# Attention and a bilinear feed-forward on one core: six passes instead of four transpose their exponentials on TensorE

## The chip, the core and the metric

One core of a Trainium2 chip runs the whole program. Its engines work side by side, each through its own queue in order: TensorE (PE; its weight loads are listed as PEld), VectorE (DVE), ScalarE (ACT), GpSimd (POOL), and SyncE (SP), which issues the transfers. The metric is the device time of one execution in microseconds. The kernel before takes 824.36 us (median of three runs, 823.71 to 825.22).

## The reference

```python
# q, k, v: (4, 8, 1152, 64) float32; two neighbouring query rows are averaged
q_pool = q.reshape(4, 8, 576, 2, 64).mean(axis=3)
scores = np.matmul(q_pool, k.transpose(0, 1, 3, 2)) / 8
attn = np.exp(scores - scores.max(-1, keepdims=True))
attn = attn / (attn.sum(-1, keepdims=True) + 1e-9)
x = np.matmul(attn, v)                      # (4, 8, 576, 64) -> 2304 tokens x 512
out = ((x @ w_a) * (x @ w_b)) @ w_out       # w_a, w_b: 512 x 1536, w_out: 1536 x 512
```

Everything is float32 at the interface. Inside, most factors of a product are split into a high and a low float16 part, and three of the four partial products are summed.

## The kernel before

**Passes.** Heads are handled in pairs, four pairs to a batch. A pass takes one pair through a set of query rows. In the first batch the rows are divided: passes 0 to 3 take pairs 0 to 3 through the 256 "even" tokens, passes 4 to 7 take pairs 3, 2, 1, 0 through the remaining 64 + 256 "rest" and "odd" tokens. In the other three batches a pass takes a pair through all 576 rows. A pass consists of units: two blocks of 128 query rows, one for each head, or a single narrow block in which 64 rows of either head share the 128 partitions. Passes 0 to 3 have two full units, passes 4 to 7 a narrow one and two full ones.

**A block.** `qk` forms 1152 scores a row on TensorE into the PSUM area `sps` (L699). `sm_max` on VectorE brings them to the tile `s` with the row maximum (L734), `sm_exp` on ScalarE takes the exponential and its sum (L741), `sm_sum` and `sm_rec` on VectorE give the reciprocal. There are two ways on from there.

**The float16 way** (passes 4 and later): `sm_hi` (ScalarE, L754) and `sm_lo` (VectorE, L758) write the normalised row as two float16 parts, a DMA transposes both (L763), and `pv` (L857) multiplies the 9 chunks of 128 keys with the split V, 54 matmuls for a full unit and 54 half as wide for a narrow one. V is split once a pass by `v_hi` (ScalarE, L541) and `v_lo` (VectorE, L544).

**The float32 way** (passes 0 to 3, `ps_.pe`, set by `n < N_PE`): `tr_pe` transposes the exponentials on TensorE, a chunk of 128 x 128 at a time, four chunks (or two, in the last part) to a part, into one of the two PSUM banks `ab0`, `ab1` (L776). `tr_out` brings each part back to SBUF, by turns on ScalarE (L787) and VectorE (L789). `pv_f` multiplies with the unsplit float32 V into the bank `xps` (L820); this shows as 36 matmuls for a full unit. `r_diag` (ScalarE, L792) puts the reciprocals on a diagonal, `r_wide` (TensorE, L796) spreads them over the partitions, also into `xps`, and `x_copy` (L870) and `r_mul` (L800) make the output of the unit. `xps` is one resource: a unit's products, the next unit's products and the sums of the weights' magnitudes go through it one after another.

**Weights.** `prep_w(f)` prepares one of 12 slices f of the three weight matrices: load, `w_abs` (L573) and `w_tail` (L592) on ScalarE, `w_sign` on GpSimd (L596), `w_join` on VectorE, a magnitude (`w_mag`, on ScalarE for odd f, L582), a sum over partitions on TensorE (`w_sum`, L615), and the high and low parts (`w_hi` L639, `w_lo` L643, L648, L652). The preparation is entered with the passes: three slices after each of passes 0 to 3 (`W_PASSES`).

**Expert tiles.** `moe_tile(t)` takes 256 tokens through the feed-forward: for each f two groups of 12 matmuls into `ab0` or `ab1` (`moe_mm`, L944), scaled and multiplied by `moe_a` (L951) and `moe_g` (L956), then a split by `moe_gh` (ScalarE, L961) and `moe_gl` (GpSimd, L964) and the output product (`moe_o`, L983). Tile 0 needs the even tokens of the first batch, whose last part comes from `x_hi` and `x_lo` of pass 3 (ScalarE L894, GpSimd L898). The banks `ab0` and `ab1` are also those of the transposes.

**What sets the order.** The body only enters tasks, by `add`, each with the tiles it reads and writes; a task is known by its number in the order of entry. `ORDERS` holds five lists, written out, that give each engine's sequence of task numbers, in the order TensorE, VectorE, ScalarE, GpSimd, SyncE; `Plan.order` merges them, and the instructions are issued in that sequence. An engine never passes over a task that waits. In the lists of before, task 491 is `x_hi` of pass 3 (172nd on ScalarE), tasks 579 and 575 are the first two products of expert tile 0 (103rd and 104th on TensorE), and task 24 is the first exponential.

## Time and profile before

| | |
|---|---|
| profiled execution | 824.24 us, span 822.5 us |
| TensorE busy | 781.4 us (95%), granted clock 0.980 on the mean |
| VectorE, ScalarE, GpSimd busy | 615.6, 581.6, 248.2 us |
| chain that ended last | TensorE 75%, ScalarE 9%, VectorE 9%, DMA 3% |

The 40 slices of the page, 20.6 us each, in tenths of a slice; PEclk is the clock that TensorE was granted, in tenths of 2.4 GHz:

```profile
PE   8887569999999999999999999999999999999997
DVE  5988999887799889999998999989887433022110
ACT  6999989877877878887987788788857442233212
PEclk9989789999999999999999999999999999999999
```

A row of the timeline gives the start in us, the time of the merged instructions, engine, line, operation, output <- inputs, the count, and in brackets the idle time before with what ended it. Matmul ends are modelled and successive instructions overlap a little, so the price of an operation is read from its start to the start of the next one. After the last matmul some 4 us are left for the last copy and store, and the profiled execution's time is 1.74 us above its span.

### The profile page before, as it was taken

What the parts mean: (1) busy time and instruction counts of PE and PEld (TensorE: products, weight loads), DVE (VectorE), ACT (ScalarE), POOL (GpSimd) and SP (SyncE); (2) the same over time, 40 slices, a digit from 0 to 9 for tenths busy, and PEclk for the clock granted to TensorE, in tenths of its full rate; (3) what the DMA queues carried; (4) which work ended last, traced back from release to release, by engine and by line L of the source; (5) the groups of instructions that cost most, each with busy time, mean ns of one, the idle gap of its engine ahead of it and who ended that gap; (6) DMA issues with size and microseconds to landing.
All of it is one profiled execution on the core that took longest, in us unless ns stands there. A gap on an engine that the chain in (4) does not pass through costs nothing.

```text
span 822.5 us, 21332 instructions
## 1 busy us (share of the span) xinstructions
PE 781.4 (95%) x8880; PEld 604.8 (74%) x8880; DVE 615.6 (75%) x1180; ACT 581.6 (71%) x986; POOL 248.2 (30%) x226
## 2 busy tenths in 40 slices
PE   8887569999999999999999999999999999999997
PEld 5664347776777767778778777887688788888886
DVE  5988999887799889999998999989887433022110
ACT  6999989877877878887987788788857442233212
POOL 5668866234201133211232023101310230311203
PEclk9989789999999999999999999999999999999999
DMA  8555698999999999999999989999968414000100
GB/s 300 209 198 174 198 212 245 190 214 218 203 202 220 208 190 190 204 212 192 190 215 203 174 177 168 209 162 213 161 117 154 88 43 100 2 27 1 27 2 26
DMA packets 316433, 132.32 MB, mean 161 GB/s; under 512 B 300848, under 2 KB 302896, under 8 KB 316336
## 3 DMA queue, kind: packets, MB, share of 16 engines
q1 hardware_dynamic: 316336, 130.96, 76.5%
q8 instruction: 69, 1.13, 0.5%
q14 instruction: 28, 0.23, 0.1%
HBM read 50.72 MB, written 4.72 MB: 67 GB/s over the span
## 4 chain that ended last, share of the span: by engine, by line
PE 75%; ACT 9%; DVE 9%; DMA 3%; issue 2%; POOL 0%; SPq 0%; ACTq 0%; DVEq 0%
PE ab L944 32%; PE ab L983 11%; PE xps L857 10%; PE sps L699 8%; PE sps L702 7%; PE sps L983 3%; DVE s L734 3%; DMA pt<-p 2%; ACT s L741 2%; DVE p L758 2%; ACT p L754 1%; PE xps L820 1%; PE xps L983 1%; ACT pt L787 1%; DMA xt<-in_w_ab_dram 1%
## 5 line engine op out<-in xcount | busy, mean ns | idle before, releaser
L944 PEld LDWEIGHTS <-wab 128*128 128x128 f16 x2592 | 251.4, 98 | 31.6 <-issue 0.9
L944 PE MATMUL ab<-xt,wab 128*128 128x256 f16 x2304 | 260.5, 273 | 0.6 <-DVE g L956 0.4
L741 ACT ACTIVATE s<-s,st 128x1152 f32<-128x1152 f32 x144 | 179.9, 1249 | 28.0 <-DVE s L734 27.2
L758 DVE SCALAR_TENSOR_TENSOR p<-s,st,p 128x1152 f16<-128x1152 f32 x128 | 183.6, 1438 | 15.3 <-ACT p L754 14.8
L754 ACT ACTIVATE p<-s,st 128x1152 f16<-128x1152 f32 x128 | 159.2, 1249 | 41.6 <-DMA pt<-p 14.4
L964 POOL TENSOR_TENSOR gl<-g,gh 128x256 fp32r<-128x256 f32 x108 | 90.0, 838 | 319.6 <-ACT gh L961 292.3
L699 PE MATMUL sps<-k,q 64*128 64x512 f32 (+3 forms) x448 | 101.5, 546 | 12.6 <-DVE s L734 6.5
L951 ACT ACTIVATE g<-ab,cc 128x256 f32<-128x256 f32 (+1 forms) x144 | 55.0, 415 | 82.6 <-PE ab L944 82.0
L734 DVE TENSOR_SCALAR_CACHE_REDUCE s<-sps,ksc 128x1152 f32<-128x1152 f32 x72 | 101.0, 1409 | 12.7 <-PE sps L702 12.2
L857 PEld LDWEIGHTS <-vs 128*64 128x64 f16 x3888 | 100.4, 110 | 13.6 <-issue 11.6
L956 DVE SCALAR_TENSOR_TENSOR g<-ab,cc,g 128x256 f32<-128x256 f32 (+1 forms) x144 | 55.3, 410 | 73.6 <-ACT g L951 73.3
L857 PE MATMUL xps<-pt,vs 128*64 128x128 f16 (+1 forms) x3888 | 109.1, 215 | 1.3 <-DMA pt<-p 1.0
L983 PE MATMUL ab<-wo,gh 128*128 128x512 f32 x336 | 108.9, 405 | 0.0
L734 DVE TENSOR_SCALAR_CACHE_REDUCE s<-sps 128x1152 f32<-128x1152 f32 x72 | 96.7, 1349 | 14.5 <-PE sps L699 13.8
L699 PEld LDWEIGHTS sps<-k,q 64*128 64x128 f32 (+1 forms) x448 | 47.1, 183 | 66.9 <-issue 50.9
L961 ACT ACTIVATE gh<-g 128x256 fp32r<-128x256 f32 x108 | 43.9, 411 | 52.8 <-PE ab L983 28.8
L983 PEld LDWEIGHTS ab<-wo,gh 128*128 128x128 f32 x336 | 60.4, 188 | 13.5 <-ACT gh L961 0.3
L983 PE MATMUL ab<-wo,gl 128*128 128x512 f32 x168 | 66.6, 396 | 1.0 <-POOL gl L964 1.0
L702 PE MATMUL sps<-k,q 64*128 64x512 f16 (+3 forms) x624 | 65.6, 341 | 1.9 <-DVE s L734 1.6
L702 PEld LDWEIGHTS <-q 64*128 64x128 f16 (+1 forms) x720 | 36.9, 97 | 41.0 <-issue 8.3
L596 POOL TENSOR_SCALAR xt<-xt 128x512 f16<-128x512 f32 x22 | 52.3, 2378 | 26.3 <-ACT xt L592 21.3
L424 POOL TENSOR_TENSOR q<-qraw 128x576 f32<-128x576 f32 (+2 forms) x20 | 28.0, 1402 | 61.0 <-DMA qraw<-in_q_dram 23.4
(135 smaller groups left out, 809.6 us busy)
## 6 DMA issues: line engine op xcount, KB each, us to landing
k<-in_k_dram SPq DMA_DIRECT2D x18, 576.0 KB, 4.4
vraw<-in_v_dram SPq DMA_DIRECT2D x17, 576.0 KB, 4.8
xt<-in_w_ab_dram SPq DMA_DIRECT2D x15, 512.0 KB, 3.9
qraw<-in_q_dram SPq DMA_DIRECT2D x12, 576.0 KB, 4.8
out_dram<-o SPq DMA_DIRECT2D x16, 256.0 KB, 2.9
xt<-in_w_out_dram SPq DMA_DIRECT2D x7, 512.0 KB, 3.9
g<-in_w_ab_dram SPq DMA_DIRECT2D x5, 512.0 KB, 3.2
wab<-in_w_ab_dram SPq DMA_DIRECT2D x4, 512.0 KB, 3.8
```

The costliest lines, as they stand in the source:

```text
L699: nc.tensor.matmul(out, q, k, start=True, stop=True)
L702: nc.tensor.matmul(out, q[:, hq], k[:, hk], start=(hq, hk) == (0, 0), stop=(hq, hk) == (1, 0))
L734: nc.vector.tensor_scalar(out=s_t[sbuf(i)], in0=sps[:, at:at + S], scalar1=-1.0 / 16.0 if u is None else ksc[:, u, 4:5], scalar2=None, op0 ...
L741: nc.scalar.activation(out=s, in_=s, func=AF.Exp, scale=-1.0, bias=t[:, 0:1], accum_out=t[:, 1:2])
L754: nc.scalar.activation(out=p_t[pbuf(i)][:, 0], in_=s_t[sbuf(i)], func=AF.Copy, scale=st_t[i % NST][:, 3:4])
L758: nc.vector.scalar_tensor_tensor(out=p[:, 1], in0=s, scalar=st_t[i % NST][:, 3:4], in1=p[:, 0], op0=ALU.mult, op1=ALU.subtract)
L857: nc.tensor.matmul(xps[half(e), at:at + w], vs[:, c, e, hv], pt[t][:, hp, c, c0:c0 + w], start=(c == 0 and n == 0), stop=(c == NCH - 1 and ...
L944: nc.tensor.matmul(dst if t < 8 else dst.rearrange("p (b n) -> p b n", b=B), wab[:, f, 1 - m, a, c], moe_x(t, b, c), start=(n == 0), stop= ...
L951: nc.scalar.activation(out=g_t[:, f, c], in_=ab[j][:, 1, c], func=AF.Copy, scale=cc[:, b, f, 0:1])
L956: nc.vector.scalar_tensor_tensor(out=g, in0=ab[j][:, 0, c], scalar=cc[:, b, f, 1:2], in1=g, op0=ALU.mult, op1=ALU.mult)
L964: nc.gpsimd.tensor_tensor(out=gl_t[j], in0=g_t[:, f], in1=gh_t[j].bitcast(F32), op=ALU.subtract)
L983: nc.tensor.matmul(out_bank(t, u), g[:, us], wo[:, f, a], start=(first and n == 0), stop=(last and n == 2))
```

## The change

`N_PE` goes from 4 to 6: passes 4 and 5 take the float32 way too. These have narrow units, so `r_wide`, `r_mul`, `moved` and `pv_f` get a width: a narrow unit has one block, nine chunks in three parts (ScalarE, VectorE, ScalarE bring them back), a product 64 columns wide, and a spread 64 wide. The spread reciprocals move from column 256 of `xps` to column 336 (`R_AT`). Pass 4 uses the float32 V of pair 3, which is still in `vraw`; pass 5 loads that of pair 2 into the place of the split V. The weights are entered over six passes, two slices with each. Tile 0 is entered after pass 5 (`m + 1 >= N_PE`), tile 1 after pass 7 as before. `moe_gl` of tiles 6, 7 and 8 is done on VectorE instead of GpSimd (`GL_DVE`). All five lists of `ORDERS` are new, and so are the numbers of the tasks: `x_hi` of pass 3 is now 413 (207th on ScalarE), the last eviction of pass 5 is 663, right behind it; the first products of tile 0 are 724 and 728 (145th and 146th on TensorE), and between them and the second halves stand 664 and 665, the last product and spread of pass 5. Of `ORDERS`, only lines with these numbers are shown.

```diff
@@ -25,12 +25,14 @@
 NF = DFF // 128
 NT = B * NQ
 P_SCALE = 2.0 ** 14
+R_AT = 336
 
 REMN = 64
 CC_F = 4
 IDLE = 8
 K_PART = 640
-N_PE, EVICT = 4, "ADADA"
+GL_DVE = (6, 7, 8)
+N_PE, EVICT = 6, "ADADA"
 N_WHOLE, TWO_ROUNDS = 2, (0,)
 
 XE, XR, XO = 0, 256, 320
@@ -52,164 +54,166 @@
 DMA_START, DMA_END, LOAD_LAG = 0.72, 0.63, 0.8
 Z_ALL, R_ALL = 30, 30
 W_KEY = (4, 1.3)
-W_PASSES = 4
+W_PASSES = 6
 PE_TICK, PE_WARM, PE_TURN, PE_STAY = 3.413, 1.275, 0.11, 0
 
 
 ORDERS = (
...
-        461, 462, 487, 488, 732, 508, 579, 575, 740, 580, 576, 750, 583, 584, 587, 534, 588, 758, 592, 593, 596, 597,
...
+        662, 638, 639, 836, 724, 728, 664, 665, 729, 725, 682, 846, 732, 736, 854, 733, 737, 871, 741, 742, 880, 745,
...
-        504, 702, 497, 433, 476, 463, 513, 725, 470, 431, 428, 489, 710, 491, 501, 507, 512, 524, 427, 728, 520, 734,
...
+        626, 620, 671, 594, 413, 663, 824, 590, 640, 647, 830, 678, 592, 653, 838, 677, 666, 833, 668, 687, 730, 726,
...
@@ -397,7 +401,7 @@
     vf = [vs.rearrange("p c e h d -> p (c e h d)").bitcast(F32).rearrange("p (c n) -> p c n", c=NCH), vraw]
 
     def vbuf(p):
-        return (["vsh", "vsl"], ["vraw"])[p % 2] if p < N_PE else ["vraw"]
+        return (["vsh", "vsl"], ["vraw"])[p % 2]
 
     pl = Plan()
     add = pl.add
@@ -528,7 +532,7 @@
         )
 
     def folds(ps_):
-        return ps_.p % NP == NP - 1 or ps_.p < NP and not ps_.pe
+        return ps_.p % NP == NP - 1 or ps_.p < NP and "odd" in ps_.parts
 
     def v_cc(b):
         nc.vector.tensor_scalar(
@@ -545,8 +549,9 @@
             out=vs[:, :, :, 1], in0=v_heads, scalar=vsc[:, p, 0:1], in1=vs[:, :, :, 0], op0=ALU.mult, op1=ALU.subtract
         )
 
-    def prep_vmax(p, new, key):
-        j = p % 2 if new and p < N_PE else 1
+    def prep_vmax(ps_, new, key):
+        p = ps_.p
+        j = p % 2 if ps_.pe else 1
         names = ["vraw"] if j else ["vsh", "vsl"]
         add("SP", 2.05, key - 3, load_v, (p, j), w=names, lag=LOAD_LAG)
         if new:
@@ -791,34 +796,39 @@
     def r_diag(i, e):
         nc.scalar.activation(out=diag[e], in_=ident, func=AF.Copy, scale=st_t[i % NST][:, 3:4])
 
-    def r_wide():
+    def r_wide(w):
         for e in range(2):
-            nc.tensor.matmul(xps[half(e), 256:384], one.broadcast_to([128, 64]), diag[e], start=True, stop=True)
-
-    def r_mul(j, x0):
-        x = x32[j][:, x0:x0 + 128]
+            d = diag[e] if w == 128 else diag[0][:, half(e)]
+            nc.tensor.matmul(xps[half(e), R_AT:R_AT + w], one.broadcast_to([128, 64]), d, start=True, stop=True)
+
+    def r_mul(j, x0, w):
+        x = x32[j][:, x0:x0 + w]
         nc.vector.scalar_tensor_tensor(
-            out=x, in0=x, scalar=1.0 / P_SCALE, in1=xps[:, 256:384], op0=ALU.mult, op1=ALU.mult
+            out=x, in0=x, scalar=1.0 / P_SCALE, in1=xps[:, R_AT:R_AT + w], op0=ALU.mult, op1=ALU.mult
         )
 
     def moved(ps_, i0, u):
-        parts = [[(i, c + d) for d in range(4)] for i in (i0, i0 + 1) for c in (0, 4)] + [[(i0, 8), (i0 + 1, 8)]]
+        both = (i0,) if u is None else (i0, i0 + 1)
+        parts = [[(i, c + d) for d in range(4)] for i in both for c in (0, 4)] + [[(i, 8) for i in both]]
+        u = u or 0
         out = []
         for n, chunks in enumerate(parts):
             j, w, on = (n + u) % 2, len(chunks), EVICT[n]
             of = sorted(set(i for i, _ in chunks))
-            name = f"pt{blocks[i0].slot}x{n}"
-            out.append(name)
+            names = [f"pt{blocks[i].slot}x{c // 4}" for i, c in chunks[::4 if w == 4 else 1]]
+            out += names
             add("PE", 0.04 + 0.11 * w, i0 - 6, tr_pe, (chunks, j), r=[f"s{sbuf(i)}" for i in of] + ["g0"], w=[f"acc{j}"])
-            add("ACT" if on == "A" else "DVE", (0.477 if w == 4 else 0.42) if on == "A" else (0.59 if w == 4 else 0.4), i0 - 3.5, tr_out, (chunks, j, on),
-                r=[f"acc{j}"], w=[name])
+            add("ACT" if on == "A" else "DVE", (0.477 if w == 4 else 0.42 if w == 2 else 0.25) if on == "A" else (0.59 if w == 4 else 0.4 if w == 2 else 0.2), i0 - 3.5, tr_out, (chunks, j, on),
+                r=[f"acc{j}"], w=names)
         return out
 
     def pv_f(p, at, slots):
+        w = 128 if len(slots) > 1 else REMN
         for c in range(NCH):
             for e in range(2):
+                c0 = 0 if len(slots) > 1 else REMN * e
                 nc.tensor.matmul(
-                    xps[half(e), at:at + 128], vf[p % 2][:, c, 64 * e:64 * e + 64], ptf[slots[e]][:, c],
+                    xps[half(e), at:at + w], vf[p % 2][:, c, 64 * e:64 * e + 64], ptf[slots[e % len(slots)]][:, c, c0:c0 + w],
                     start=(c == 0), stop=(c == NCH - 1),
                 )
 
@@ -880,7 +890,7 @@
         add("ACT", 0.072 + 0.192 * w / 256 + 0.08 * (ps_.pe or fold), key - 4, x_copy, (j, at, x0, w, ps_.p, ps_.pe, fold),
             r=["xps"] + [f"vb{ps_.p // NP}" if fold else f"vsc{ps_.p}"] * (ps_.pe or fold), w=[f"x32{j}{c}" for c in range(x0 // 64, (x0 + w) // 64)])
         if ps_.pe:
-            add("DVE", 0.2, key - 4, r_mul, (j, x0), r=["xps"], w=[f"x32{j}{c}" for c in range(x0 // 64, (x0 + w) // 64)])
+            add("DVE", 0.2, key - 4, r_mul, (j, x0, w), r=["xps"], w=[f"x32{j}{c}" for c in range(x0 // 64, (x0 + w) // 64)])
 
     def x_parts(p, j, which, hl):
 
@@ -960,8 +970,8 @@
     def moe_gh(f, j):
         nc.scalar.activation(out=gh_t[j], in_=g_t[:, f], func=AF.Copy)
 
-    def moe_gl(f, j):
-        nc.gpsimd.tensor_tensor(out=gl_t[j], in0=g_t[:, f], in1=gh_t[j].bitcast(F32), op=ALU.subtract)
+    def moe_gl(f, j, dve):
+        (nc.vector if dve else nc.gpsimd).tensor_tensor(out=gl_t[j], in0=g_t[:, f], in1=gh_t[j].bitcast(F32), op=ALU.subtract)
 
     sums_in = {}
 
@@ -1025,7 +1035,8 @@
             j = len(outs) % NG
             outs.append((t, f))
             add("ACT", 0.31, key - 20, moe_gh, (f, j), r=[f"g{f}"], w=[f"gh{j}"])
-            add("POOL", 0.7, key - 20, moe_gl, (f, j), r=[f"g{f}", f"gh{j}"], w=[f"gl{j}"])
+            dve = t in GL_DVE
+            add("DVE" if dve else "POOL", 0.36 if dve else 0.7, key - 20, moe_gl, (f, j, dve), port=True, r=[f"g{f}", f"gh{j}"], w=[f"gl{j}"])
             add("PE", 1.405, key - 1, moe_o, (t, f, j, f == 0, f == NF - 1),
                 r=[f"gh{j}", f"gl{j}", f"w{f}2h", f"w{f}2l"], w=sorted({out_name(t, u) for u in range(2)}), mode=3)
         for u in range(2):
@@ -1109,7 +1120,7 @@
     for n in range(IDLE):
         add("PE", 0.44, -40 if n < 8 else 2 * (n - 8), idle, (), r=["ones"], w=["xps"])
     prep_qk(passes[0], -20)
-    prep_vmax(0, True, -10)
+    prep_vmax(passes[0], True, -10)
 
     def attend(m):
         ps_ = passes[m]
@@ -1131,13 +1142,13 @@
                 block(ps_, i)
                 i += 1
             if r == 1 and nxt and not nxt.again:
-                prep_vmax(nxt.p, nxt.parts[0] == "even", ps_.end - 4)
+                prep_vmax(nxt, nxt.parts[0] == "even", ps_.end - 4)
             if ps_.pe:
-                parts = moved(ps_, i - 2, r)
-                add("PE", 2.02, i - 10, pv_f, (ps_.p, at, tuple(slots)), r=[f"pt{t}" for t in slots] + parts + vbuf(ps_.p),
+                parts = moved(ps_, i - 2, r) if w == 128 else moved(ps_, i - 1, None)
+                add("PE", 2.02 if w == 128 else 1.06, i - 10, pv_f, (ps_.p, at, tuple(slots)), r=[f"pt{t}" for t in slots] + parts + vbuf(ps_.p),
                     w=["xps"], mode=2)
-                add("PE", 0.3, i - 10, r_wide, (), r=["g1", "g2", "ones"], w=["xps"], mode=2)
-                leaving = [(at, XE + at, 128)]
+                add("PE", 0.3 if w == 128 else 0.17, i - 10, r_wide, (w,), r=["g1", "g2", "ones"] if w == 128 else ["g1", "ones"], w=["xps"], mode=2)
+                leaving = [(at, ps_.q0 + at, w)]
             else:
                 unit(slots, at, w, i - 1)
             for span in leaving:
@@ -1157,15 +1168,15 @@
             if ps_.p // NP == b:
                 attend(m)
                 if m < W_PASSES:
-                    weights(NF // W_PASSES * m, NF // W_PASSES * (m + 1))
-                if m == W_PASSES:
+                    weights(NF * m // W_PASSES, NF * (m + 1) // W_PASSES)
+                if m == W_PASSES - 1:
                     add("POOL", 0.4, ps_.base, kz_zero, (), w=["z2", "kz0", "kz1"], port=False)
                 if b and "even" in ps_.ends:
                     add("DVE", 0.1, NBLK * NP * b, v_cc, (b,), r=[f"wsc{f}" for f in range(NF)] + [f"vb{b}"],
                         w=[f"cc{b}{f}" for f in range(NF)])
                 for n in ps_.ends:
                     late.append(2 * b + (n == "odd"))
-                if b in TWO_ROUNDS:
+                if b in TWO_ROUNDS and m + 1 >= N_PE:
                     while late:
                         moe_tile(late.pop(0))
         while late and late[0] < 2 * b:
```

## Rows read from the trace of the kernel before

**Rows 1.** Busy time by stretch: length, PE, PEld, DVE, ACT, POOL, clock, DMA.

```profile
20.00:30.00 10.00, 9.60 (x88) 7.04 (x84) 9.61 (x25) 10.00 (x24) 3.48 (x3) 1.00 0.52 174
...
9.90:83.70 73.80, 62.19 (x465) 43.20 (x464) 66.20 (x145) 70.42 (x146) 54.64 (x29) 0.93 0.62 219
83.70:127.70 44.00, 28.12 (x224) 18.93 (x224) 42.28 (x87) 41.79 (x77) 34.90 (x18) 0.77 0.84 209
...
121.90:190.00 68.10, 66.81 (x886) 51.26 (x886) 61.22 (x109) 58.91 (x95) 25.90 (x19) 1.00 1.03 216
...
600.00:818.00 218.00, 218.00 (x2075) 184.53 (x2073) 71.97 (x168) 84.32 (x187) 42.39 (x56) 1.00 0.25 48
```

**Rows 2.** Timeline of PE: the first product of expert tile 0.

```profile
121.91 2.78 PE L944 MATMUL ab<-xt,wab 128*128 128x256 f16 x24
```

**Rows 3.** Timeline of ACT and POOL: first exponential, split of pass 3.

```profile
10.05 1.26 ACT L741 ACTIVATE s<-s,st 128x1152 f32<-128x1152 f32 x1 [0.28 <-DVE s L734]
...
119.98 0.41 ACT L894 ACTIVATE xt<-x 128x256 f16<-128x256 f32 x1
...
121.24 0.82 POOL L898 TENSOR_TENSOR xt<-x,xt 128x256 f16<-128x256 f32 x1
```

**Rows 4.** Timeline of PE in passes 0 and 1.

```profile
19.12 2.17 PE L699 MATMUL sps<-k,q 64*128 64x512 f32 x10 [0.16 <-issue]
21.23 1.09 PE L776 MATMUL ab<-g,s 128*128 128x128 f32 x8
22.25 2.19 PE L820 MATMUL xps<-pt,vs 128*64 128x128 f32 x36
24.27 0.39 PE L796 MATMUL xps<-g,one 128*64 128x128 f32 x4
24.59 0.44 PE L776 MATMUL ab<-g,s 128*128 128x128 f32 x2
24.96 0.48 PE L699 MATMUL sps<-k,q 64*128 64x128 f32 x2
25.37 0.66 PE L776 MATMUL ab<-g,s 128*128 128x128 f32 x4
```

**Rows 5.** Timeline of PE: a narrow and a full unit the float16 way.

```profile
155.65 1.04 PE L857 MATMUL xps<-pt,vs 128*64 128x64 f16 x54
156.62 1.48 PE L944 MATMUL ab<-xt,wab 128*128 128x256 f16 x12
...
164.62 1.70 PE L857 MATMUL xps<-pt,vs 128*64 128x128 f16 x54
166.25 2.15 PE L699 MATMUL sps<-k,q 64*64 64x512 f32 x12
```

**Rows 6.** Timeline of ACT in passes 3 and 4.

```profile
83.72 1.25 ACT L741 ACTIVATE s<-s,st 128x1152 f32<-128x1152 f32 x1
...
84.96 0.68 ACT L573 ACTIVATE wab<-wab 128x512 f32<-128x512 f32 x1
85.55 0.57 ACT L787 ACTIVATE pt<-ab 128x512 f32<-128x512 f32 x1
86.03 0.67 ACT L573 ACTIVATE o<-xt 128x512 f32<-128x512 f32 x1
86.60 0.39 ACT L792 ACTIVATE g<-g,st 128x128 f32<-128x128 f32 x1
86.89 0.66 ACT L592 ACTIVATE xt<-xt 128x512 int32<-128x512 uint32 x1
...
88.28 0.37 ACT L870 ACTIVATE x<-xps,vsc 128x128 f32<-128x128 f32 x1
88.53 0.67 ACT L573 ACTIVATE o<-xt 128x512 f32<-128x512 f32 x1
89.08 1.26 ACT L754 ACTIVATE p<-s,st 128x1152 f16<-128x1152 f32 x1
90.22 0.63 ACT L639 ACTIVATE wo<-o 128x512 fp32r<-128x512 f32 x1
```

286 rows, old and new, of the table ORDERS are left out of this document.

## The prediction

> **What bounds the kernel now.** I read the page's 40 slices first. From the seventh slice on TensorE stands at 9 and its clock at full speed; before that it stands at 5 to 8, while ScalarE and VectorE stand at 8 and 9. So there are two stages, and the table by stretch gives their limits. In the opening, from the first exponential to about 128 us, ScalarE is busy 70.42 + 41.79 = 112.2 of 117.8 us (95.3%), VectorE 66.20 + 42.28 = 108.5, TensorE 62.19 + 28.12 = 90.3, and part of that at 1.2 GHz: the granted clock is 0.93 and then 0.77 [rows 1]. From 121.9 to 190 us TensorE is busy 66.81 of 68.10 us at the full clock, at the end 218.0 of 218.0 [rows 1]. The border is the first product of expert tile 0, at 121.91 [rows 2]: behind it TensorE always has something to do.
>
> For this kernel that gives a simple account. Behind the first product of tile 0 the time is the sum of what then stands in TensorE's queue. In front of it the time is ScalarE's: that product needs the last part of x, which pass 3 splits on ScalarE at 119.98, and its low part on GpSimd, 0.82 from 121.24 [rows 3]. The change moves work from behind this border to in front of it, and it moves the border. The question is by how much each.
>
> **What leaves the queue behind the border.** TensorE's lists show it directly. Three scores, three remainders of scores and all six float16 units of passes 4 and 5 stood behind the first product and now stand in front of it (the units in their float32 form). Scores take 19.12 to 21.23 = 2.11 us, a remainder 24.96 to 25.37 = 0.41 [rows 4]; a full float16 unit 164.62 to 166.25 = 1.63, a narrow one 155.65 to 156.62 = 0.97 [rows 5]. That is 3 x 2.52 + 4 x 1.63 + 2 x 0.97 = 16.0. Only the last product of pass 5 and its spread stand behind the border anew: 22.25 to 24.27 = 2.02, and 24.27 to 24.59 = 0.32 [rows 4]. Net 16.0 - 2.3 = 13.7 us. So the change pays if the border moves by less than 13.7 us, to before 135.6.
>
> **What TensorE gets in all.** A full float32 unit costs four parts of four chunks at 0.51 (eight chunks take 21.23 to 22.25), one of two at 0.37, the product 2.02 and the spread 0.32: 4.75, against 1.63, so +3.12. The narrow unit is not in the trace. Its transposes are 2 x 0.51 and one chunk (0.13 to 0.37, I take 0.2); its product lies between half of the full one and all of it (1.01 to 2.02), and since the narrow float16 unit takes 0.97/1.63 of the full one I take 1.2; its spread lies between 0.16 and 0.32, I take 0.2: 2.6 in all, +1.65. Four and two of them make +15.8 (15.2 to 18.0) [rows 4, 5]. Nearly all of it stands in front of the border, where TensorE is not the limit. At full clock the work there was 62.19 x 0.93 + 28.12 x 0.77, less the 5.8 us behind the border: 73.7 [rows 1]. Now come 7.6 of scores, three full products with spreads (7.0), the transposes of four full units (9.6) and two narrow units (5.2): 103.1. If the border is near 136.7, that is 103 in 126.7 us: the cover holds if the mean granted clock of the opening is above 0.81.
>
> **What ScalarE gets in front of the border.** I counted its two lists from the first exponential to the split of pass 3. Prices are from start to start [rows 6]. Exponentials 22 to 27, 5 x 1.24 = 6.2. The float16 high parts, five of p and one of V, go: 6 x 1.14 = -6.8. Diagonals 16 to 24, 8 x 0.29 = 2.3. Four-chunk evictions 16 to 26, 10 x 0.48 = 4.8. Small evictions 8 to 13; I price them like the diagonal, 1.5 (0.25 to 0.48 each, 1.3 to 2.4). Copies of x 8 to 12, 4 x 0.25 = 1.0. One more split of x, of two parts, 0.6. Weights: 90 instructions to 99, 9 x 0.57 = 5.1. Sum +14.7. So although the passes themselves get cheaper for ScalarE, the border now waits for five more blocks and almost one more slice of weights. At the busy share of 95.3% [rows 1] this is 15.4 us: the split of pass 3 moves from 119.98 to 135.4. Its low part then starts about 0.4 later (before it stood behind another GpSimd instruction) and takes 0.82: the border comes at 136.6, which is 14.7 later than 121.91. The last eviction of pass 5, which frees the bank for the first product, stands right behind the split in the list and ends in the same half microsecond.
>
> **What I cost at nothing.** VectorE sheds ten low parts of p and two of V, and gains ten evictions and six products; it was less busy than ScalarE and stays so. Ten DMA transposes go; the DMA share was 0.62 to 0.84 there [rows 1], so no wait goes with them. The V of pass 5 goes to the other buffer, but is loaded as before. Each new product, spread, copy and multiplication goes through the one bank `xps`: behind a product that waits there stand, on TensorE, the scores of later blocks, and for these wait VectorE's maxima and ScalarE's exponentials. Passes 0 to 3 have the same chain, and its waits are inside the 4.7% that I keep; if it costs more, see the third rival. The subtractions of tiles 6 to 8 go to VectorE in a stretch where it is busy 72 of 218 us and TensorE never waits [rows 1]: no gain, no loss. Behind the border ScalarE still has weights to prepare: to the magnitude that the twelfth slice's sum needs are 5 exponentials, 6 high parts, 15 weight instructions and some 4 us of small ones, 25.6, at 95.3% 26.9: at 162.3. TensorE has 24.3 in front of that sum, and would be there at 160.9: a wait of some 1.4 us, against 1.29 us of idle that the stretch from 121.9 to 190 had [rows 1]. I count them as equal; the bounds are -2 and +4.
>
> **Sum.** The border +14.7, the queue behind it -13.7: +1.0. From the profiled execution's own 824.24 that gives 825.2 us; it was 0.12 below the median of the runs, 824.36.
>
> **The rivals.**
>
> First, ScalarE is held less, and the border comes early enough: faster. Of the way to the split of pass 3, some 5.2 us were idle. For it: VectorE was nearly as full, and it is what sheds work, so the waits on it could go; the new lists are another interleaving altogether. Against: TensorE, whose transposes ScalarE now waits for in six passes instead of four, gets fuller. If all the idle time goes, the border comes at 136.6 - 5.2 - 0.7 = 130.7, and the time is 819.3. It decides as soon as two thirds of it go: 136.6 - 4 is some 822.
>
> Second, the clock, which ends slower. Between 83.7 and 127.7 TensorE ran at a granted 0.77 [rows 1], that is nearly half the time at 1.2 GHz, after the idle stretches of a stage in which ScalarE set the pace. If the whole opening has that clock, 103.1 of work need 133.9 us, TensorE becomes the bound of its own border, which comes at 143.9, and the time is 832.5. It decides below 0.81, as worked out above. Against it: passes 0 to 3 did this kind of work at 0.93, and the stretch from 20 to 30 us, with transposes in it, at 1.00 [rows 1]; in the low stretch TensorE had little to do, and that is where the new work goes. The Trainium skill ("TensorE: Matmul & The Clock Gate", Part 4: PE-mode transpose) says that the full clock does not come on for transposes. By that rule the 90 new ones would run at 1.2 GHz and the clock would drop in passes 4 and 5; the trace of before does not agree, with its 1.00 between 20 and 30 us.
>
> Third, the chain through `xps` and the two banks holds ScalarE more than in passes 0 to 3, because six units instead of none now lie in the stretch behind 83.7. If its idle share doubles there, over some 53 us, the border comes 2.6 later: 827.8.
>
> **How the numbers follow.** A change of 0.2%, 1.65 us, is about what a measurement of this kernel can tell from none: below 822.7 is faster, above 826.0 slower. My forecast, ScalarE sets the border at its old busy share: 0.42, with a range of its own of 822.3 to 827.5 (its busy share two points either way; 0.03 of it faster, 0.25 the same, 0.14 slower). The first rival 0.34, all of it faster; the second 0.12 and the third 0.12, slower. Together: faster 0.37, same 0.25, slower 0.38. The range takes in the first rival with two microseconds less idle behind the border, and below the second's full price: 817.5 to 832.
>
> **What would show it.** In the profile after, the first L944 at 136 to 137, the pass 3 split (L894) 1.2 before it, ScalarE busy 95% up to there, and a granted clock above 0.86 in the opening show the steps right. L776 should have 234 matmuls instead of 144 and L754 118 instead of 128. The border before 133 with ScalarE busy 98% is the first rival; TensorE busy without a gap in the 50 us before its border, at a clock below 0.8, the second; ScalarE waiting for L796, L776 or L870's inputs the third. The account as a whole is wrong if the shift of the border less 13.7 is not the change in time: then the difference lies in waits behind the border, and the table by stretch will show where.

## The result: 0.8% slower, and the profile after

| | before | after |
|---|---|---|
| median of 5 runs | 824.36 us | 831.22 us |
| lowest to highest | 820.69 to 827.19 | 827.14 to 832.97 |
| ratio, 95% interval | | 1.0076, 1.0048 to 1.0103 |
| profiled execution, its span | 824.24, 822.5 | 832.97, 830.9 |

The time lies in the range (817.5 to 832), but the forecast of about the same time does not hold: the kernel got 6.9 us slower, the forecast was 0.8. The profiled execution of after is the longest of its five runs; the account below is of that execution (span +8.4). Two executions stand far out, 997.87 us of `tail_as_before` (an experiment below) and 1553.39 us of the kernel before in the second of the four sets there: the medians given hold them, the ratios do not.

The border first. The table of after by stretch (length, then PE, PEld, DVE, ACT, POOL, clock, DMA), with the opening, the 68.1 us behind the border, and the end, for [rows 1], and behind it the opening of before up to its own border:

```profile
10.17:138.10 127.93, 112.23 (x968) 76.75 (x968) 114.24 (x254) 121.16 (x259) 90.47 (x49) 0.93 0.55 192
138.10:206.20 68.10, 67.18 (x817) 50.88 (x817) 63.86 (x115) 59.40 (x98) 23.44 (x17) 1.00 1.00 212
...
600.00:818.00 218.00, 217.47 (x2226) 181.83 (x2224) 100.93 (x228) 94.11 (x198) 16.16 (x21) 1.00 0.34 62
```
```profile
10.00:121.91 111.91, 84.43 (x640) 57.33 (x640) 103.25 (x221) 106.82 (x213) 85.16 (x44) 0.86 0.69 212
```

Timelines of after: ScalarE's split of pass 3 and GpSimd's low part, for [rows 3]; TensorE's first product of tile 0 with what stands just ahead of it, for [rows 2]; and the new narrow float32 product, of which no row was to be had before:

```profile
135.97 0.41 ACT L904 ACTIVATE xt<-x 128x256 f16<-128x256 f32 x1
```
```profile
136.45 0.67 POOL L908 TENSOR_TENSOR xt<-x,xt 128x256 f16<-128x256 f32 x1 [1.82 <-ACT xt L904]
```
```profile
106.47 1.27 PE L830 MATMUL xps<-pt,vraw 128*64 128x64 f32 x36
107.57 0.29 PE L802 MATMUL xps<-g,one 128*64 128x64 f32 x4
...
124.98 4.10 PE L704 MATMUL sps<-k,q 64*64 64x512 f32 x12 [1.75 <-POOL q L428]
...
135.36 2.19 PE L830 MATMUL xps<-pt,vs 128*64 128x128 f32 x36 [0.35 <-DVE x L806]
...
138.11 2.79 PE L954 MATMUL ab<-xt,wab 128*128 128x256 f16 x24
```

The border moved by 16.2 us, from 121.91 to 138.11; 14.7 had been predicted. With the 13.7 us that left the queue behind it this makes +2.5, and a span of 825.0. The span is 830.9. The other 5.9 us came up behind the border. From here on I call that difference, span - (822.5 + shift of the border - 13.7), the **excess** of a run.

The table by stretch finds it. The next two fences have the same three stretches behind the border, of before and of after, and the third has the last of them for a kernel from the experiments (`after_to_p13`), with the same columns:

```profile
121.91:200.00 78.09, 75.81 (x972) 57.06 (x971) 67.89 (x119) 66.69 (x108) 32.67 (x25) 1.00 1.04 219
200.00:300.00 100.00, 98.51 (x1220) 73.75 (x1218) 84.91 (x152) 76.91 (x114) 19.17 (x21) 1.00 1.09 203
...
345.00:435.00 90.00, 88.73 (x1226) 68.74 (x1224) 86.54 (x153) 75.26 (x113) 18.37 (x19) 1.00 1.12 203
```
```profile
138.11:200.00 61.89, 61.55 (x747) 46.80 (x748) 58.24 (x106) 55.57 (x93) 23.43 (x17) 1.00 0.99 214
200.00:300.00 100.00, 99.42 (x1161) 73.61 (x1158) 86.24 (x157) 74.38 (x112) 20.44 (x23) 1.00 1.07 194
...
345.00:435.00 90.00, 84.61 (x1142) 64.96 (x1141) 81.34 (x148) 69.75 (x105) 21.20 (x20) 0.96 1.03 197
```
```profile
345.00:435.00 90.00, 88.27 (x1144) 69.30 (x1141) 77.11 (x137) 66.79 (x104) 16.60 (x19) 1.00 0.96 183
```

The idle time of TensorE is length less busy time. Up to 300 us before had 2.3 + 1.5 = 3.8 us of it, after has 0.3 + 0.6 = 0.9: the new lists are better there by 2.9. From 345 to 435 us before had 1.3, after has 5.4, and its clock is 0.96 instead of 1.00, worth an estimated 0.04 x 90 = 3.6 us. Nearly the whole loss lies in those 90 us: 4.1 + 3.6 - 2.9 makes 4.8 of the 5.9 us, and some 0.8 more are short waits behind 435 us. TensorE's timeline of after shows the place: two waits, 4.85 us in sum, and behind each of them work at a lower clock: 53 products of p and V take 2.95 us instead of 1.67, a score 2.81 instead of 1.62:

```profile
401.88 1.62 PE L707 MATMUL sps<-k,q 64*128 64x512 f16 x15
...
416.80 2.95 PE L867 MATMUL xps<-pt,vs 128*64 128x128 f16 x53 [2.58 <-DMA pt<-p]
...
430.31 2.81 PE L707 MATMUL sps<-k,q 64*128 64x512 f16 x15 [2.27 <-DVE s L739]
...
499.76 1.67 PE L867 MATMUL xps<-pt,vs 128*64 128x128 f16 x53 [1.74 <-DMA pt<-p]
```

VectorE in the same place (the timeline of after) is without a gap up to 417.8 and then stands still for 3.83 us, because the score that it needs next is queued on TensorE behind the product that waits for the transposes:

```profile
421.68 1.42 DVE L739 TENSOR_SCALAR_CACHE_REDUCE s<-sps,ksc 128x1152 f32<-128x1152 f32 x1 [3.83 <-PE sps L707]
```

### The profile page after: what moved, and what is told of

Same layout as the page of the kernel before. It is cut to its first block, busy times and chain, and to the rows that moved or that the text cites. A ratio compares the mean times of both kernels' runs of the same rounds, so it can differ in the third digit from the quotient of the medians.

```text
span 830.9 us, 21321 instructions
## 1 busy us (share of the span) xinstructions
PE 797.9 (96%) x8886; PEld 615.8 (74%) x8886; DVE 622.0 (75%) x1220; ACT 574.6 (69%) x1008; POOL 223.0 (27%) x190
## 5 line engine op out<-in xcount | busy, mean ns | idle before, releaser
L763 DVE SCALAR_TENSOR_TENSOR p<-s,st,p 128x1152 f16<-128x1152 f32 x118 | 167.6, 1429 | 22.5 <-ACT p L759 21.8
L759 ACT ACTIVATE p<-s,st 128x1152 f16<-128x1152 f32 x118 | 146.3, 1249 | 38.2 <-DVE st L756 18.8
L974 POOL TENSOR_TENSOR gl<-g,gh 128x256 fp32r<-128x256 f32 x72 | 68.3, 955 | 226.2 <-ACT gh L971 170.4
L867 PE MATMUL xps<-pt,vs 128*64 128x128 f16 (+1 forms) x3564 | 101.8, 216 | 5.5 <-DMA pt<-p 5.2
L867 PEld LDWEIGHTS <-vs 128*64 128x64 f16 x3564 | 93.8, 111 | 16.9 <-issue 15.6
L781 PE MATMUL ab<-g,s 128*128 128x128 f32 x234 | 38.0, 292 | 8.8 <-ACT pt L792 4.9
```

The lines of the kernel that those rows point to most:

```text
L759: nc.scalar.activation(out=p_t[pbuf(i)][:, 0], in_=s_t[sbuf(i)], func=AF.Copy, scale=st_t[i % NST][:, 3:4])
L763: nc.vector.scalar_tensor_tensor(out=p[:, 1], in0=s, scalar=st_t[i % NST][:, 3:4], in1=p[:, 0], op0=ALU.mult, op1=ALU.subtract)
L867: nc.tensor.matmul(xps[half(e), at:at + w], vs[:, c, e, hv], pt[t][:, hp, c, c0:c0 + w], start=(c == 0 and n == 0), stop=(c == NCH - 1 and ...
L974: (nc.vector if dve else nc.gpsimd).tensor_tensor(out=gl_t[j], in0=g_t[:, f], in1=gh_t[j].bitcast(F32), op=ALU.subtract)
```

## The experiments

Task names: P13u4pv is the product of p and V of unit 4 of pass 13, P14b94qk the score of block 94 in pass 14, P17ksum the broadcast of a maximum in pass 17, T2f5o the output piece of slice 5 of tile 2. Each engine has one written list of such tasks. A kernel that "changes over" at a task issues everything that after's order issues before that task in that order, and all the rest in the order of before. Ratios are to the kernel before, run on the same chip in the same set of runs; its medians were 823.68, 823.78, 823.97 and 824.14 in the four sets.

| kernel | median, us | ratio (95%) | border | excess |
|---|---|---|---|---|
| after_again | 830.85 | 1.0075 (1.0054 to 1.0096) | 137.5 | +4.9 |
| tail_as_before | 824.05 | 1.0000 (0.9985 to 1.0016) | 136.0 | -0.8 |
| gl_gpsimd | 829.54 | 1.0065 (1.0046 to 1.0085) | 133.5 | +6.2 |
| tr_twice | 828.76 | 1.0062 (1.0038 to 1.0086) | 136.1 | +7.9 |
| pv13_later | 829.83 | 1.0068 (1.0043 to 1.0092) | 136.9 | +4.5 |
| pv_both_later | 833.17 | 1.0098 (1.0073 to 1.0123) | 135.4 | +9.2 |
| qk26_later | 824.46 | 1.0006 (0.9992 to 1.0020) | 137.9 | -0.5 |
| abs_twice | 825.13 | 1.0018 (1.0005 to 1.0030) | 138.5 | -0.2 |
| after_to_p13 | 821.57 | 0.9967 (0.9952 to 0.9982) | 139.6 | -3.7 |
| after_to_p15 | 830.62 | 1.0064 (1.0042 to 1.0087) | 135.3 | +3.8 |
| lo_short | 827.99 | 1.0043 (1.0022 to 1.0063) | 133.5 | +4.4 |
| tr_half | 827.14 | 1.0042 (1.0022 to 1.0061) | 137.3 | +3.1 |

Border and excess are of the profiled execution, the median of all runs of the kernel. An excess is thus one sample: in the four kernels that leave after's order behind the border as it is up to 600 us (after, after_again, gl_gpsimd, tr_twice) it lies between 4.9 and 7.9.

**Where the loss is.** `after_again` is the kernel after the change, unchanged.

> The changed kernel unaltered, for a second profile. My theory: its time is the first product of expert tile 0 (138.1 us, 16.2 later than before, fixed by ScalarE's queue and the same from run to run within 0.5), plus a queue behind it that is 13.7 shorter, plus waits of TensorE behind it and the low clock after them, which vary: the profiled run had 8.9 us of waits and two stretches at half clock. So the border comes at 138 +- 0.5 again, and the time anywhere from 827 to 833, with the difference in waits and clock between 400 and 500 us. Rival: what is slower is fixed and sits in the opening; then the border itself moves with the time.

The ratio came again (1.0075), and so did the two waits: 2.61 us at 416.72 and 2.26 at 428.64. But behind the first of them the clock stayed up this time, 1.67 us in place of 2.95:

```profile
416.72 1.67 PE L867 MATMUL xps<-pt,vs 128*64 128x128 f16 x53 [2.61 <-DMA pt<-p]
```

`tail_as_before` keeps the six passes and the new opening, changes over at the first maximum of pass 10 (some 220 us) and leaves the low halves of the last tiles on GpSimd:

```diff
-lists of after
+lists of after up to P10b54max, then the order of before
-GL_DVE = (6, 7, 8)
+GL_DVE = ()
```

> The changed kernel up to the first maximum of pass 10 (some 220 us); from there on every engine works off what is left in the order of the kernel before, and the low parts of tiles 6 to 8 are on GpSimd again. Theory: the border stays at 138, the waits behind it fall to those of before (6.5 us, no low clock after 140 us), so the time is that of before plus 16.2 less 13.7, some 827, 4 us less than the changed kernel. Rival, the loss is the work that TensorE got in addition or the opening: 831, as the changed kernel. Rival, the order behind the border makes nothing but noise: 831 and as widely spread.

It takes as long as before, excess -0.8; that is 3 us less than the theory's 827, because the border came 2 us earlier than in after and TensorE idles 6.1 us behind it, against 7.1 before. So the six passes with their border cost what the account says, next to nothing, and the loss belongs to the order behind the border. `gl_gpsimd` has only the second half of that edit:

> The changed kernel with the low parts of tiles 6, 7 and 8 on GpSimd again, in the same place of the sequence. Theory: TensorE is full there, so only its end changes: within 1 us of the changed kernel, 830 to 831 for the median. Rival: VectorE, which gets 36 subtractions, holds the maxima of the last passes; then 3 us or more come back.

Excess 6.2, and a median 1.3 us below that of after_again: the subtractions on VectorE are not it.

**The opening.** `tr_twice` issues the transposes of passes 4 and 5 twice, into the same bank, so TensorE gets some 10 us more ahead of the border:

```diff
-        for n, (i, c) in enumerate(chunks):
-            nc.tensor.transpose(acc[j][:, 128 * n:128 * n + 128], ...
+        for again in range(2 if chunks[0][0] >= 16 and len(chunks) == 4 else 1):
+            for n, (i, c) in enumerate(chunks):
+                nc.tensor.transpose(acc[j][:, 128 * n:128 * n + 128], ...
```

> The changed kernel with every four-chunk part of passes 4 and 5 transposed twice: 20 parts of 0.51 us, 10.2 us more on TensorE in front of the border, same result. Theory, TensorE is covered there by ScalarE: the border comes at most 2 us later (each eviction waits half a microsecond longer, but ScalarE has other work in its queue), time +0 to +2. Rival, the added TensorE work is what the change pays for: the border comes 8 to 10 us later and the time is about 840.

The border stayed within what it varies by, far from the 8 to 10 us of the rival, so most of TensorE's share of the change is covered, as predicted. Not all of it: gl_gpsimd, with the same granted clock in the opening and without the added work, has its border at 133.5, 2.5 us earlier. The table by stretch of this kernel from 10 us to its border:

```profile
10.00:136.07 126.07, 114.61 (x1048) 83.31 (x1047) 111.60 (x254) 121.88 (x260) 87.52 (x49) 0.99 0.59 197
```

Eighty more float32 transposes, and the granted clock is 0.99. `abs_twice` adds to ScalarE instead, on the base of tail_as_before:

```diff
-        nc.scalar.activation(out=z_t[zi(n)], ..., func=AF.Abs, scale=2.0 ** -112)
+        for _ in range(2 if 18 <= n < 24 else 1):
+            nc.scalar.activation(out=z_t[zi(n)], ..., func=AF.Abs, scale=2.0 ** -112)
```

> The same kernel (824.05), in which six of the weights' magnitudes on ScalarE (experts 6 and 7) are computed twice, ahead of the border: 6 x 0.57 us = 3.4 us more on ScalarE, the output is unchanged. Theory (ScalarE sets the border at 95% busy, and what the border loses the end loses): border 135.96 + 2.5 to 3.4 = 138.5 to 139.4, time 826.5 to 827.5. Rival (ScalarE has slack where it waits 2.6 us for transposes just ahead of the border): border 136 to 137, time 824 to 825.

The border went to 138.5, 2.5 later, but the median only rose by 1.1 us: between the two expectations. The next kernel, without the added work, has its border at 137.9 at the same granted clock of the opening, 0.93. The kernel after (138.1) and tr_half (137.3), with the opening lists unaltered and at 0.93 too, have theirs in the same place. Only a small part of what ScalarE gets arrives at the border. `qk26_later`, on the same base, moves one score out of the way on TensorE (P5u0pvf is the float32 product of unit 0 of pass 5):

```diff
-... W9.1wsum P6b26qk P5u2tr0 P5u0pvf P5u0rwide P5u2tr2 ...
+... W9.1wsum P5u2tr0 P5u0pvf P6b26qk P5u0rwide P5u2tr2 ...
```

> The kernel with the six passes in the opening, the order of before behind it and the low halves of the last three tiles on GpSimd (824.05 in the earlier run), with one edit: in TensorE's list the first scores of the first float16 pass (P6b26qk) stand behind the last transposes of P5u2's first chunk and the narrow product P5u0pvf, no longer ahead of them. Theory (TensorE's 1.76 us wait for q on GpSimd at 122 to 124, half-clock scores of 3.6 us behind it and ScalarE's 2.6 us wait for the transposes behind those are a loss on the path to the border): ScalarE's wait at 125.4 falls below 1 us, the border comes 1.5 to 2.5 us earlier (133.5 to 134.5), time 822 to 822.8, below the kernel before. Rival (ScalarE's sum and the later products set the border anyway, the first maxima of pass 6 come later and hold it): border 135.5 to 136.5, time 824.

A miss, and the rival's account: ScalarE waits 4.3 us for a later maximum in place of 2.6 for the transposes, and the time is the same.

**Which wait it is.** My theory was one misplaced product, P13u4pv, too early in TensorE's list.

```diff
-... P13u2pv P13u3pv P13u4pv P14b94qk T2f5o P14b95qk ...
+... P13u2pv P13u3pv P14b94qk T2f5o P13u4pv P14b95qk ...
```

> The kernel after the change with one edit: in TensorE's written list the last attention product of pass 13 stands one score block and one output piece later (behind P14b94qk and T2f5o). Theory (the loss is two waits that the new order behind the border puts at 414 to 430 us, with the low clock that follows them): the 2.6 us wait of the attention product for the transposed p at 416.8 and the 2.3 us wait of the scores at 430.3 go, the clock in 400 to 440 is back near 1.00, the border stays at 136 to 138; the excess of the span over 822.5 + shift of the border - 13.7 falls from 5.9 to about 1 to 2, time 825 to 827. Rival (the moved border piece or VectorE's new load is what costs, and the waits only come up a few us later): waits behind the border stay at 8 to 9 us, excess 5 to 6, time 829 to 831.

The theory fell. In TensorE's timeline of pv13_later the wait for the transposes is gone and the clock is up, but three other waits of 5.0 us in sum stand in the same stretch:

```profile
416.06 1.65 PE L679 MATMUL sps<-k,q 64*64 64x512 f16 x18 [1.99 <-DVE s L711]
...
426.47 0.73 PE L965 MATMUL ab<-wo,gh 128*128 128x512 f32 x2 [2.23 <-ACT gh L943]
...
429.41 1.62 PE L679 MATMUL sps<-k,q 64*128 64x512 f16 x15 [0.77 <-DVE s L711]
```

The second edit of the kind, at 500 us, did not help:

```diff
-... P15u3pv P15u4pv P16b112qk P17ksum T3f0o P16b113qk ...
+... P15u3pv P16b112qk T3f0o P15u4pv P17ksum P16b113qk ...
```

> As the run before, and the last attention product of pass 15 also one score block and one output piece later (behind P16b112qk and T3f0o; the maximum's broadcast P17ksum goes behind it, since both write the same PSUM bank). Theory: the 1.7 us wait at 499.8 goes too; excess 0 to 1, time 823.5 to 826, 1 to 2 us below the run before. Rival: TensorE is not what sets the pace at 500 (VectorE waits 2 us for scores there anyway): no difference to the run before.

The wait at 499.8 goes and four of 0.7 to 0.8 us stand in its place. The median is 3.3 us above that of pv13_later, but the intervals of the two ratios overlap, and the excess of 9.2 is not the edit's alone: up to 435 us the two kernels have the same lists and the same three waits (here 2.07, 2.23 and 0.65), and behind the last of them the clock fell here and stayed up there:

```profile
427.61 3.04 PE L679 MATMUL sps<-k,q 64*128 64x512 f16 x15 [0.65 <-DVE s L711]
```

Then two changes of order as a whole. Both have GL_DVE = () and change over at another task: `after_to_p13` at P13b81max (some 345 us), `after_to_p15` at P15b99max (some 435 us).

> The written lists of the kernel after the change up to the first maximum of pass 13 (some 345 us), behind it the order of before, low halves of the last three tiles on GpSimd. Where the order changes over, the products of tile 2 that before's lists have had by then come in a bunch among the scores of pass 13. Theory (the loss is made at 400 to 500 us, where the lists of after give VectorE 97 to 98% of work and TensorE no expert product to do meanwhile; the order up to 345 us is as good as before's): border 133.5 to 138, TensorE waits at 400 to 500 us about 2 us as in the run with before's order from pass 10, excess of the span over 822.5 + shift of the border - 13.7 between -1 and +1, time 822 to 825. Rival (the loss is laid down earlier, by the expert products of tile 1 that stand later in after's lists than in before's at 220 to 345 us, and only shows at 400): excess 4 to 6, time 828 to 830.

> The same with the change-over at the first maximum of pass 15 (some 435 us): the stretch with the waits of 2.6 us at 416.8 and 2.3 us at 430 and the low clock between them is after's, that with the wait of 1.7 us at 499.8 is before's. Theory: the first two waits stand as in after and cost with the low clock 4 to 6 us, the third is gone: excess 3 to 5, time 826.5 to 829. Rival (the waits there are recovered later, the loss is made behind 435 us): excess 0 to 1, time 823 to 825.

With the stretch from 345 to 435 us in before's order the excess is -3.7; with the same stretch in after's it is +3.8, with both waits where they were:

```profile
414.69 1.67 PE L839 MATMUL xps<-pt,vs 128*64 128x128 f16 x53 [2.65 <-DMA pt<-p]
426.62 3.03 PE L679 MATMUL sps<-k,q 64*128 64x512 f16 x15 [2.26 <-DVE s L711]
```

So the stretch is settled: the two kernels differ by 9 us in the median. `after_to_p13` lies below what its theory gave (time 822 to 825, excess -1 to +1). It is also faster than both kernels, before and after, by 0.33% (0.18 to 0.48) against before, although its border is the latest of all, 139.6.

**Who is late.** In after VectorE has no gap from 390 us to 417.8. `lo_short` takes work from it (the low halves of five blocks are left out but for 128 columns):

```diff
+        n = 128 if 84 <= i < 89 else S
         nc.vector.scalar_tensor_tensor(
-            out=p[:, 1], in0=s, ..., in1=p[:, 0], ...
+            out=p[:, 1, 0:n], in0=s[:, 0:n], ..., in1=p[:, 0, 0:n], ...
```

> The kernel after the change, in which the low half of p is computed on VectorE over the first 128 of 1152 columns for the five blocks 84 to 88 of pass 13 (the rest of these low halves is left out, so the output differs): 5 x some 1.2 us = 6 us less on VectorE between 385 and 417 us; TensorE's lists and work are unchanged. Theory (VectorE is what paces the stretch: moving one product of pass 13 only moved the wait): the waits at 416.8 and 430.3 fall from 4.8 to under 1.5 us in sum and the low clock at 415 to 435 goes, border 135.5 to 138, time 824.5 to 827. Rival (TensorE's own order or the DMA transposes set the waits, whatever VectorE does): both waits stand within 0.7 us of 2.6 and 2.3, time 829 to 831.

Both waits stand, 2.25 and 2.27 us, though VectorE now has gaps; the lower time of the profiled execution goes with its early border, 133.5, not with the waits. The low half of block 89, the last that the waiting product needs, was written 7.3 us before the wait ended (405.13 to 412.44; in after 409.44 to 416.80). The queue's timeline of after has six transposes there in one row; the second fence is the view of that line (ns of each: least, median, most; and us from issue to landing):

```profile
399.79 20.47 SPq L768 DMA_TRANSPOSE pt<-p  x6
```
```profile
L768 SPq DMA_TRANSPOSE pt<-p x6: 2709/3052/3475, 399.8 to 417.6; - x6
DMA to landing us min/median/max: 4.6/6.1/6.9
```

The queue is nearly full, but 1.6 of the 20.47 us are its own waits for low halves from VectorE. The transpose of block 89 is issued at 410.51, 1.1 us after the low half was written, and lands 6.2 us later: most of the 7.3 us is the transfer, not the wait for its turn.

`tr_half` takes work from that queue (the low halves of the same blocks are not transposed, old contents are used):

```diff
-            out=pt[blocks[i].slot].rearrange(...), in_=p_t[pbuf(i)].rearrange(...),
+            out=pt[blocks[i].slot][:, 0:1 if 84 <= i < 89 else 2].rearrange(...),
+            in_=p_t[pbuf(i)][:, 0:1 if 84 <= i < 89 else 2].rearrange(...),
```

> The kernel after the change, in which the transposes of p for the five blocks 84 to 88 of pass 13 carry the high halves alone (the low halves' old contents are used, so the output differs): five transposes of some 3.3 us on SP's queue become half as long, 5 to 8 us less on that queue between 390 and 417 us; TensorE's and VectorE's work and order are unchanged. Theory (after VectorE's relief changed nothing: the last product of pass 13 waits for the queue of transposes, in which the last block lands 7.3 us after VectorE has written it): the wait at 416.8 falls from 2.6 to under 0.8 us, the second at 430 from 2.3 to under 1 since VectorE is not left idle before it, border 133.5 to 138, excess of the span over 822.5 + shift of the border - 13.7 falls to 0 to 2, time 824.5 to 827. Rival (the chain from the last scores of pass 13 through maximum, exponential and both halves is too long for the expert products that TensorE has meanwhile, whatever the queue does): both waits within 0.7 us of 2.6 and 2.3, excess 4 to 6, time 828 to 831.

Both old waits go, as the theory says (the second is 0.39 now): block 89, itself transposed whole, lands 4.6 us after its low half is written. A new one of 2.76 us for ScalarE's high half of an expert product takes their place, with the low clock behind it:

```profile
424.64 0.73 PE L993 MATMUL ab<-wo,gh 128*128 128x512 f32 x2 [2.76 <-ACT gh L971]
...
427.41 2.77 PE L707 MATMUL sps<-k,q 64*128 64x512 f16 x15 [0.39 <-DVE s L739]
```

The excess is 3.1, between the two expectations. The medians of tr_half and lo_short are some 3 us below after's; how much of that is owed to the waits, and how much to the border, is not shown.

The product was moved, VectorE relieved, the queue relieved, and each time the same or another wait of 2 us and more stood in the stretch. What these kernels have in common is TensorE's own list. The table by stretch from the score of blocks 90 and 91 to that of blocks 97 and 98, seven blocks in each kernel, in this order before, after_to_p13, pv13_later, lo_short and tr_half:

```profile
410.81:441.71 30.90, 29.77 (x411) 22.90 (x410) 28.84 (x51) 24.74 (x38) 8.77 (x11) 1.00 1.14 218
```
```profile
412.36:442.68 30.32, 29.70 (x411) 22.92 (x412) 28.48 (x51) 24.40 (x38) 8.75 (x11) 1.00 1.09 204
```
```profile
401.78:429.41 27.63, 22.50 (x327) 16.07 (x327) 23.79 (x40) 19.63 (x32) 10.60 (x11) 1.00 0.92 176
```
```profile
397.85:424.37 26.52, 22.00 (x328) 15.93 (x328) 21.64 (x36) 19.58 (x32) 10.51 (x10) 1.00 0.96 193
```
```profile
401.44:427.41 25.97, 22.72 (x327) 16.35 (x327) 23.68 (x40) 19.73 (x32) 9.50 (x11) 0.98 0.84 163
```

In before and in after_to_p13 TensorE (first figure behind the length) has 29.7 us of work between these two scores, more than VectorE (third) with 28.5 to 28.8. In after's order it has 22.0 to 22.7, VectorE 23.7 to 23.8: the new lists have some 7 us fewer expert products there. But these sums are not the whole of it. The queue needs only an estimated 7 x 3.05 = 21.4 us for its seven blocks, and in lo_short VectorE has 21.6, no more than TensorE, and 4.5 us of waits stand.

What fits lo_short too is the way from a score to the product that needs it: maximum, exponential, both halves, transpose. From the last part of the score of blocks 88 and 89 to their product, in before, in after (its product is the row at 416.80 above) and in lo_short:

```profile
401.54 0.34 PE L702 MATMUL sps<-z,q 128*128 128x128 f16 x3
...
425.97 1.67 PE L857 MATMUL xps<-pt,vs 128*64 128x128 f16 x53 [1.00 <-DMA pt<-p]
```
```profile
392.78 0.34 PE L707 MATMUL sps<-z,q 128*128 128x128 f16 x3
```
```profile
388.80 0.34 PE L707 MATMUL sps<-z,q 128*128 128x128 f16 x3
...
412.44 1.67 PE L868 MATMUL xps<-pt,vs 128*64 128x128 f16 x53 [2.25 <-DMA pt<-p]
```

The way takes 24.4, 24.0 and 23.6 us, about the same in all. Less the wait, TensorE's list has 23.4 us of work for that time in before and 21.4 in the other two, and the wait is what is missing. With the second wait it is the same. The next two fences have the last part of the score of blocks 95 and 96 and the score of 97 and 98 behind it, in before and in after (there it is the row at 430.31 above):

```profile
436.20 0.34 PE L702 MATMUL sps<-z,q 128*128 128x128 f16 x3
...
441.71 1.63 PE L702 MATMUL sps<-k,q 64*128 64x512 f16 x15
```
```profile
424.73 0.34 PE L707 MATMUL sps<-z,q 128*128 128x128 f16 x3
```

They stand 5.5 and 5.6 us apart. Before's list has work for all of it, after's for 3.3 us.

That the order of this stretch decides is shown by the two change-overs. That it does so because the new list has too little work between a score and what follows from it is read from these rows. tr_half, which shortened the way, bears it out for the first wait; no kernel added work to the list there.

## Why the prediction was right in part and wrong in the sum

- **The queue behind the border, 13.7 us shorter: right.** tail_as_before has its border 14.05 us later than before; less 13.7 that gives a span of 822.85, measured 822.0, and TensorE's idle time behind the border was 1.0 us shorter.
- **ScalarE +14.7: right.** From 10 us to the border it was busy 106.8 us before and is busy 121.2 now, +14.4.
- **TensorE covered: nearly.** In tr_twice another 10 us move the border by 2.5 us at the same granted clock. The narrow product took 1.10 from start to start against my 1.2.
- **The border, 136.6: 1.5 us early.** The split of pass 3 came at 135.97 against 135.4, and the border 2.1 us behind it instead of 1.2. The low part was done at 137.12; from 135.36 to 138.11 TensorE worked without a gap on a product, a spread and a remainder that stand in front of the border, so at the end TensorE did set it. In before the low part was not the last to come either: by [rows 3] it was done at 122.06, and the border at 121.91 stood right behind a sum (121.66) that had waited 1.27 us for a magnitude from ScalarE. The other part that failed is "ScalarE sets the border at its old busy share": with the same opening lists the border lay between 133.5 and 139.6 in the runs, along with the clock that TensorE was granted (last section). A miss of 1.5 us is less than that.
- **The step that failed is "I count them as equal; the bounds are -2 and +4"**, the waits behind the border. I looked at 121.9 to 190 us alone, where the new order is in fact better, and took the 250 us behind for fixed. The change rewrites the order there too: fewer expert products among the scores of passes 13 and 14, two waits of 4.85 us, and the low clock behind them. That is the excess of 5.9 us in place of 0, above the bound, and 5.9 of the 8.4 us of span.
- **The range, 817.5 to 832: held by luck.** The range of the forecast itself ended at 827.5. The time, 831.22, lies inside the wider one because the second rival's price had drawn its upper end, and that rival did not come.
- **The first rival** (border 130.7) happened in no run; the nearest are 133.5. Its sum has a slip: four microseconds off the 825.2 are 821.2, not "some 822", and 822.7 is passed with half of the idle time, not two thirds. **The second** gave 832.5, close to the time measured, and is still wrong: its mechanism needs the opening at 0.77, and it had 0.93 in after and 0.92 to 0.99 in the others. The rule named beside it (the Trainium skill, "TensorE: Matmul & The Clock Gate", Part 4: PE-mode transpose: the full clock does not engage for transposes) does not agree with these traces: 0.99 with 80 more transposes in the opening. **The third**, a chain through `xps` that holds ScalarE, put 2.6 us on the border. The sign for it came: ScalarE waited 4.5 us for transposes, where before it had waited 0.2. But 3.5 of them are one wait for transposes that stood on TensorE behind a score waiting for q on GpSimd (124.98), not behind a product in `xps`.
- **The subtractions on VectorE at no cost: right.** TensorE is busy 217.47 of 218 us at the end, and taking them back (gl_gpsimd) did not help.

The prediction named its own test: if the shift of the border less 13.7 is not the change in time, the difference lies in waits behind the border and the table by stretch shows where. That test found it.

What stays open: how much of the two waits each step on the way from a score to its product is worth was not separated; why the clock falls behind a wait in one execution and not in the next; and why after_to_p13 gains 1 us more than its idle time explains (4.4 us behind the border against 7.1 before, an excess of -3.7).

## What to carry to other kernels

When a change comes with a new order of the work, predict the order as a change of its own: for each stretch between two scores add up the own work of TensorE's list and that of each engine and queue that feeds it, and for each product that needs a score compare TensorE's work between the two with the time that the way between them takes (here 21.4 us of work for 24). A wait that goes when one instruction is moved and comes back elsewhere in the same stretch points to work that is missing there, not to a misplaced instruction. Join the good half of the new order to the old one before discarding either: here the new order up to 345 us and the old behind it beat both.

## What the runs showed of the hardware

The border followed the clock that TensorE was granted in the opening, with the same lists. The table by stretch from 10 us to the border, in this order gl_gpsimd, after_again and after_to_p13:

```profile
10.00:133.52 123.52, 106.91 (x968) 74.75 (x969) 113.72 (x254) 120.99 (x259) 89.57 (x49) 0.99 0.59 198
```
```profile
10.00:137.51 127.51, 111.13 (x968) 76.61 (x969) 115.28 (x256) 121.24 (x259) 89.94 (x49) 0.95 0.57 193
```
```profile
10.00:139.57 129.57, 113.97 (x968) 78.19 (x968) 115.26 (x254) 120.96 (x259) 89.54 (x49) 0.92 0.56 189
```

ScalarE's busy time is the same within 0.3 us, yet the border moves by 6 us between the clocks 0.99 and 0.92. An opening that ScalarE fills to 93 to 98% still pays for TensorE's clock, because ScalarE waits for the transposes once the clock is down. The place where it shows best is the score at 124.98 in the timeline of after: behind the same wait for q it took 4.10 us there and 2.15 in lo_short, whose border is at 133.5, and ScalarE's wait for the transposes behind it was 3.5 and 1.1 us:

```profile
122.77 2.15 PE L704 MATMUL sps<-k,q 64*64 64x512 f32 x12 [1.76 <-POOL q L428]
```

That is 2.4 of the 6 us; the rest was not followed. I had put the border down to ScalarE alone.

And a short wait can cost twice: behind the one of 2.58 us, on a TensorE that was otherwise full, the next products ran partly at the lower clock (2.95 us in place of 1.67), and the two waits of 4.85 us in sum came with a mean clock of 0.96 over 90 us. Not always: in after_again the same wait, 2.61 us, left it up (1.67), and with the same three waits in the same lists the clock stayed at 1.00 in pv13_later and fell in pv_both_later (a score in 1.62 and in 3.04 us).
